# Inverting the sums of the feature maps on ScalarE instead of GpSimd, a start in two halves, and new thresholds in a planned two-part attention kernel

## The chip, the cores and the metric

One core of one Trainium2 chip. The metric is the device time of one launch in microseconds, the median of several runs. Engines are named as in the profile: PE is TensorE, DVE is VectorE, ACT is ScalarE, POOL is GpSimd, and SP is SyncE, whose queue issues nearly all transfers.

## What is computed

Two independent attention layers on inputs of 2048 tokens and 512 features, with 32 heads of 16 features each. The results are laid side by side.

```
# part A: softmax attention
q, k, v = split(x @ wqkv)
p = softmax(q @ k.T / 4)
a = (p @ v) @ wo
# part B: linear attention with a learned feature map
pq, pk = q @ w_phi, k @ w_phi                  # per head, 16 x 16
phi = concat([softmax(pq), softmax(-pq)])      # 16 + 16 features, likewise for pk
kv, z = phi_k.T @ v, sum(phi_k)
b = (phi_q @ kv) / (phi_q @ z + 1e-6) @ wo
out = concat([a, b], -1)
```

## The kernel before

**The planner.** The program is written out by a planner that runs while the kernel is built (`_Account`, L116). It keeps an account of when each engine is free, by costs written into the code (`act_cost`, `dve_cost`, and pairs such as `(1.95, 1.95 + PLAT)` for one task), and at each point of its own time `K.now` it chooses the next instruction for each engine: `pick_pe` (L1927) for PE, `choose` (L1985) for ACT, DVE, POOL and SP, by priority. What comes out is one fixed list for each engine, run in order, with semaphore waits between them (`_Plan.emit`). So an instruction that waits holds up all that stands behind it on its engine, and the costs decide only the order, not the time on the chip.

**Part A** is the bulk. It goes in 73 units (`units`, L230): a group of four heads by 256 (some 128) queries. For each unit the scores are computed twice:

- *D*: scores with the queries on the partitions (`d_fill`, L1041; its matmuls are L971), in PSUM banks of 512 columns. DVE takes the maximum of one or of two banks at once (`tensor_reduce`, L1084), two when a pair of neighbouring banks was free.
- The maxima of a unit are joined (POOL, L1116 to L1122), turned by a transfer and put into spare rows of the masked queries `QZ`, which POOL makes (L915).
- *E*: scores again with the keys on the partitions (`e_fill`, L1215; matmuls L1234), now with the maximum subtracted by the matmul itself. ACT takes the exponential of one or two banks into the ring `pT` (L1246).
- `pv_run` (L1299) multiplies the ring by the values (L1324). `finish_unit` copies the result to `X` (L560), inverts the sums on DVE (L1384) and spreads them by transfers; POOL multiplies (L1403).

A few D items (*z*) are shared: ACT does a relu of 1024 columns (L1011) and DVE a custom instruction (L1078).

**Copies out of PSUM** go through `evac` (L554): some only to ACT, the others to ACT or DVE, whichever is free first. `choose` lets DVE have such a copy only when the work that DVE has left is at most what ACT has left plus the threshold `BAL`.

**The thresholds** (`TH0`, L409, with a row of `TH` for each 60 us of the planner's time) steer `pick_pe`. `SINGLE` is the backlog of DVE, in planned microseconds, below which D may take a single bank though two would be wanted; `ESINGLE` is the same for E on ACT. `DCAP` and `ECAP` are the backlogs above which no more is issued, `COL` and `INCOL` say when PE may turn to the other kinds of matmul, `PV_START`, `PV_LOW` and `PVN` when the ring is emptied. `UA`, `RF`, `REPM`, `LHARD` and `LHI` set how many matmuls are repeated or put in as filler, and `BAL` is told above.

**Part B** is woven into the same lists. `fm(n)` (L1556), for 16 token blocks of keys and then 16 of queries, is a chain: projection on PE, copy to `pB`, seven POOL tasks that find the maximum and minimum of each head (L1588, L1591, L1616) and subtract them, an exponential of 1024 columns on ACT (L1639, tile `eB`), the sums of 16 on POOL (L1645 to L1650, into `rB`, 64 columns of f32), their inverse, and the product `phi` on POOL (L1677). One map's `eB` is used until its `phi` is done (`e_busy`). The inverse of the sums is made by POOL itself: a first guess by integer arithmetic on the bits (L1660), and three Newton steps of three instructions (L1662 to L1664). The guess and the products lie in the tile `WQp`.

**The start.** The weights for the first heads come on ACT's queue, x on SP's in five loads (`load_x`, L328): two of 256 rows and three of 512. PE turns the first 512 rows by 16 matmuls with the identity (L374), when each of the first two loads has landed; DVE and ACT copy them to `xAT` (L381, L383), 512 columns at a time. The first projections of K and Q follow (L710), then `first_qz` (L727) masks Q for the first three units (L734, DVE), and the first D matmuls run. The planner starts its account at 7.6 us.

ACT's table of functions is loaded once, as the set `natural_log_exp_and_others` (L2040).

Of the kernel before, what the change touches and what calls it, by code (L numbers as in the profile page):

```python
# [6 lines left out]
ACT = mybir.ActivationFunctionType  # L7
# [206 lines left out]
def bass_concat_heads__softmax_full_mha__linear_kernel_hedgehog__prompt_kernel(  # L214
# [21 lines left out]
    with contextlib.ExitStack() as es:  # L236
# [91 lines left out]
        def load_x(name, b0, b1):  # L328
            t_xs[name] = P.dma("sp", dsem("xs%d" % name), lambda e: e.dma_start(
                xs[:, b0:b1, :], A_x[0][128 * b0:128 * b1, :].rearrange("(b p) n -> p b n", p=128)))  # L330
# [5 lines left out]
        load_x(2, 4, 8)  # L336
# [27 lines left out]
        t_wqp = pad_copy(WQp, 0, t_wq0)  # L364
# [5 lines left out]

        pe_idle(6, [t_zmv, t_ones])
        for rb in range(4):
            for ct in range(4):
                t_turn = P.op("pe", lambda e, rb=rb, ct=ct: e.matmul(  # L374
                    PS[:, ct, 128 * rb:128 * rb + 128], xs[:, rb, ct * 128:ct * 128 + 128], ident[:, :],
                    start=True, stop=True), [t_xs[rb // 2], t_ident] if ct == 0 else [])
        pe_idle(2)
        t_x0 = []
        for ct in range(4):
            if ct % 2 == 0:  # L380
                t_x0.append(P.op("dve", lambda e, ct=ct: e.tensor_copy(xAT[:, ct, 0:512], PS[:, ct, :]), [t_turn]))  # L381
# [20 lines left out]
        for r in range(4):  # L402
# [11 lines left out]
            {'SINGLE': 1.157, 'UA': 0.408, 'RF': 0.436, 'REPM': 0.215, 'LHI': 0.03, 'PV_START': 5, 'PV_LOW': 5, 'DCAP': 1.302, 'ECAP': 1.815, 'ZBIAS': 0.315, 'BAL': -28.613},  # L414
            {'SINGLE': 0.287, 'UA': 0.425, 'RF': 0.532, 'REPM': 0.196, 'LHARD': 0.35, 'LHI': 0.119, 'DCAP': 1.302, 'ECAP': 1.815, 'ZBIAS': 0.315, 'DBIAS': 0.27, 'BAL': -27.419},
            {'SINGLE': 1.157, 'UA': 0.408, 'RF': 0.436, 'REPM': 0.214, 'LHARD': 0.383, 'LHI': 0.03, 'PV_START': 5, 'PV_LOW': 5, 'PVN': 3, 'DCAP': 1.322, 'ECAP': 1.904, 'ZBIAS': 0.315, 'BAL': -27.335},
            {'COL': 0.708, 'SINGLE': 1.157, 'UA': 0.441, 'REPM': 0.196, 'LHI': 0.065, 'PVN': 3, 'DCAP': 2.495, 'ECAP': 1.461, 'ZBIAS': 0.315, 'DBIAS': 0.27, 'BAL': -27.419},
            {'ESINGLE': 1.165, 'RF': 0.62, 'REPM': 0.196, 'LHI': 0.065, 'ECAP': 1.185, 'ZBIAS': 0.049, 'DBIAS': 0.27, 'BAL': -27.419, 'ZREST': -0.23},
            {'ESINGLE': 1.2, 'RF': 0.62, 'REPM': 0.196, 'LHI': 0.122, 'ECAP': 1.185, 'ZBIAS': 0.049, 'DBIAS': 0.27, 'BAL': -27.419, 'ZREST': -0.23},
            {'COL': 0.63, 'INCOL': 0.753, 'ESINGLE': 1.097, 'RF': 0.436, 'REPM': 0.196, 'LHI': 0.079, 'JOBHOLD': 20.274, 'DCAP': 2.036, 'ECAP': 1.185, 'ZBIAS': 0.034, 'DBIAS': 0.314, 'BAL': -27.419, 'ZREST': -0.23},  # L420
            {'COL': 0.487, 'INCOL': 0.753, 'SINGLE': 0.633, 'ESINGLE': 1.097, 'RF': 0.596, 'REPM': 0.196, 'LHI': 0.079, 'JOBHOLD': 20.274, 'DCAP': 2.036, 'ECAP': 1.185, 'ZBIAS': 0.034, 'DBIAS': 0.334, 'BAL': -27.419, 'ZREST': -0.23},
            {'COL': 0.63, 'INCOL': 0.753, 'SINGLE': 0.663, 'ESINGLE': 1.097, 'UA': 0.458, 'RF': 0.676, 'REPM': 0.196, 'LHARD': 0.355, 'LHI': 0.246, 'JOBHOLD': 14.826, 'PV_START': 5, 'DCAP': 2.036, 'ECAP': 1.276, 'ZBIAS': 0.072, 'DBIAS': 0.278, 'BAL': -30.019, 'ZREST': -0.23},
            {'COL': 0.53, 'INCOL': 0.753, 'SINGLE': 0.674, 'ESINGLE': 1.097, 'UA': 0.442, 'RF': 0.67, 'REPM': 0.369, 'LHARD': 0.317, 'LHI': 0.259, 'JOBHOLD': 12.459, 'PV_START': 5, 'DCAP': 2.021, 'ECAP': 1.276, 'ZBIAS': 0.129, 'DBIAS': 0.278, 'BAL': -37.649, 'ZREST': -0.23},
            {'COL': 0.35, 'INCOL': 0.753, 'SINGLE': 0.749, 'ESINGLE': 1.097, 'UA': 0.433, 'RF': 0.67, 'REPM': 0.369, 'LHI': 0.259, 'JOBHOLD': 25, 'PV_START': 5, 'ECAP': 1.276, 'ZBIAS': 0.391, 'DBIAS': 0.278, 'BAL': -37.649, 'ZREST': -0.23},
# [1656 lines left out]
```

## Time and profile before

| | us |
|---|---|
| median of 3 runs | 1202.8 |
| lowest and highest of them | 1199.12, 1205.19 |
| the profiled execution | 1199.05 |
| its span, first to last instruction | 1197.3 |

The granted clock of TensorE is 0.999 of full speed over the span.

A row of a group reads: line, engine, operation, written tile <- read tiles, shape of both, count | busy us, mean ns of one | us that the engine was idle just before them, and what ended that idle time. Instructions of one engine overlap a little at their ends, so the busy time of many can be less than their count times the mean of one. A row of a timeline begins with the start and the length in us, and puts idle time and what ended it in brackets.

### The profile page before, as it was taken

What the parts mean: (1) busy time and instruction counts of PE and PEld (TensorE: products, weight loads), DVE (VectorE), ACT (ScalarE), POOL (GpSimd) and SP (SyncE); (2) the same over time, 40 slices, a digit from 0 to 9 for tenths busy, and PEclk for the clock granted to TensorE, in tenths of its full rate; (3) what the DMA queues carried; (4) which work ended last, traced back from release to release, by engine and by line L of the source; (5) the groups of instructions that cost most, each with busy time, mean ns of one, the idle gap of its engine ahead of it and who ended that gap; (6) DMA issues with size and microseconds to landing.
All of it is one profiled execution on the core that took longest, in us unless ns stands there. A gap on an engine that the chain in (4) does not pass through costs nothing.

```text
span 1197.3 us, 32106 instructions
## 1 busy us (share of the span) xinstructions
PE 1117.4 (93%) x13025; PEld 468.9 (39%) x13025; DVE 1170.3 (98%) x1290; ACT 1149.8 (96%) x1891; POOL 821.8 (69%) x1636
## 2 busy tenths in 40 slices
PE   8998999998999999999999998999999998899998
PEld 3433333343334333333433333333333333345555
DVE  8999999999999999999999999999999999999995
ACT  5898999999999999999999999999999999999997
POOL 8511211227888888888787887888888888888860
PEclk9999999999999999999999999999999999999999
DMA  5011221210002001001000101121112111111120
GB/s 142 9 25 43 42 48 32 43 38 8 8 14 35 8 6 26 13 10 22 12 7 17 25 7 22 22 49 31 29 34 33 35 34 27 20 29 37 33 30 18
DMA packets 104119, 33.61 MB, mean 28 GB/s; under 512 B 86692, under 2 KB 103972, under 8 KB 103972
## 3 DMA queue, kind: packets, MB, share of 16 engines
q1 hardware_dynamic: 102916, 31.31, 13.4%
q8 instruction: 102, 1.67, 0.6%
q14 instruction: 45, 0.37, 0.1%
q10 hardware_dynamic: 1056, 0.26, 0.1%
HBM read 5.26 MB, written 4.19 MB: 8 GB/s over the span
## 4 chain that ended last, share of the span: by engine, by line
ACT 38%; DVE 33%; PE 23%; SPq 2%; issue 1%; POOL 1%; DMA 1%
ACT pT L1246 32%; DVE part L1084 32%; PE PS L1234 7%; PE PS L971 6%; PE PS L1324 5%; PE PS L1419 2%; ACT eB L1639 1%; ACT xAT L560 1%; PE PS L777 1%; ACT zS L1011 1%; ACT X L560 1%; SPq L1392 1%; ACT WQp L560 1%; POOL uB L1588 1%; PE PS L1563 0%
## 5 line engine op out<-in xcount | busy, mean ns | idle before, releaser
L1084 DVE TENSOR_REDUCE part<-PS 128x2 f32<-128x1024 f32 (+1 forms) x1118 | 1130.0, 1079 | 7.6 <-PE PS L971 5.2
L1246 ACT ACTIVATE pT<-PS 128x512 bf16<-128x512 f32 (+1 forms) x1573 | 1027.7, 797 | 21.3 <-PE PS L1234 17.9
L1234 PE MATMUL PS<-QZ,KT 64*128 64x256 bf16 (+1 forms) x4906 | 560.4, 259 | 40.9 <-ACT pT L1246 22.0
L971 PE MATMUL PS<-KT,QZ 64*128 64x512 bf16 x2139 | 484.5, 383 | 26.3 <-DVE part L1084 9.7
L1234 PEld LDWEIGHTS PS<-QZ,KT 64*128 64x128 bf16 x4906 | 245.5, 94 | 323.1 <-ACT pT L1246 161.4
L971 PEld LDWEIGHTS PS<-KT,QZ 64*128 64x128 bf16 x2139 | 126.2, 93 | 198.2 <-DVE part L1084 72.2
L1324 PE MATMUL PS<-pT,VP 128*17 128x256 bf16 (+1 forms) x4672 | 186.7, 261 | 0.9
L1403 POOL TENSOR_TENSOR QT<-X,Yd 128x256 bf16<-128x256 f32 (+1 forms) x70 | 46.8, 668 | 95.4 <-DMA Yd<-Yd 95.1
L1324 PEld LDWEIGHTS PS<-pT,VP 128*17 128x17 bf16 x4672 | 74.9, 88 | 95.2 <-issue 79.0
L1588 POOL TENSOR_TENSOR uB<-uB 128x256 f32<-128x256 f32 (+2 forms) x160 | 83.4, 522 | 10.1
L1591 POOL TENSOR_SCALAR uB<-uB 128x256 f32<-128x256 f32 (+2 forms) x128 | 82.6, 646 | 11.2
L1116 POOL TENSOR_TENSOR dm<-part 128x16 f32<-128x16 f32 (+1 forms) x66 | 15.7, 238 | 91.1 <-DVE part L1084 90.8
L915 POOL TENSOR_TENSOR QZ<-QT,mask 128x512 bf16<-128x512 bf16 (+1 forms) x70 | 65.9, 941 | 15.7 <-PE PS L1234 12.8
L1645 POOL TENSOR_TENSOR xAT<-eB 128x512 f32<-128x512 bf16 x32 | 36.9, 1152 | 40.8 <-ACT eB L1639 40.6
L1677 POOL TENSOR_TENSOR wA<-eB,rB 128x1024 bf16<-128x1024 bf16 x32 | 61.7, 1928 | 2.0
L560 ACT ACTIVATE xAT<-PS 128x512 f32<-128x512 f32 (+3 forms) x83 | 50.1, 617 | 4.4 <-PE PS L1443 2.9
L1648 POOL TENSOR_TENSOR xAT<-xAT 128x256 f32<-128x256 f32 x64 | 36.0, 563 | 5.0
L1563 PE MATMUL PS<-WKp,xBT 128*128 128x512 bf16 x128 | 36.4, 383 | 1.1 <-ACT pT L1246 0.5
L1639 ACT ACTIVATE eB<-uB 128x1024 bf16<-128x1024 f32 x32 | 36.0, 1124 | 0.0
L1419 PE MATMUL PS<-WOp,QT 128*128 128x512 bf16 x120 | 35.8, 384 | 0.1
L1588 POOL TENSOR_TENSOR uB<-xAT,mB 128x512 f32<-128x512 f32 x32 | 33.8, 1057 | 1.8
L1662 POOL TENSOR_TENSOR WQp<-rB,WQp 128x64 f32<-128x64 f32 x96 | 30.6, 319 | 6.4
(113 smaller groups left out, 752.4 us busy)
## 6 DMA issues: line engine op xcount, KB each, us to landing
out_dram<-xAT SPq DMA_DIRECT2D x31, 128.0 KB, 1.8
Yd<-Yd SPq DMA_DIRECT2D x220, 16.0 KB, 2.1
QT<-eB SPq DMA_DIRECT2D x60, 32.0 KB, 2.0
QZ<-mcols SPq DMA_DIRECT2D x110, 1.0 KB
pT<-in_A_x_dram SPq DMA_DIRECT2D x3, 512.0 KB, 7.5
KT<-eB SPq DMA_DIRECT2D x48, 32.0 KB, 2.0
mcols<-stage SPq DMA_TRANSPOSE x69, 2.2
Yd<-Yd SPq DMA_DIRECT2D x60, 8.0 KB, 1.9
```

What stands on the lines that cost most here:

```text
L560: return P.op("act", lambda e: e.activation(dst, src, ACT.Copy), tk)
L915: "pool", lambda e: e.tensor_tensor(QZ[:, u % NQZ, :, 0:w], QT[:, g, q0:q0 + w].unsqueeze(1).broadcast_to([128, 2, w]), mask2[:, 0, :].uns ...
L971: return e.matmul(PS[:, b, :], QZ[p:p + 64, u % NQZ, r % 2, qt * 128:qt * 128 + 128], KT[p:p + 64, g, kc * 512:(kc + 1) * 512], start=star ...
L1084: tk = P.op("dve", lambda e: e.tensor_reduce(o, banks_ap(banks), AX.X, ALU.max), dep)
L1234: tok = P.op("pe", lambda e, r=rs[k], b=banks[k], kt=kt, x=x: e.matmul(PS[:, b, x * w:(x + 1) * w], KT[64 * (r // 2):64 * (r // 2) + 64, g ...
L1246: tk = P.op("act", lambda e: e.activation(pT[:, s0:s0 + n, :] if n > 1 else pT[:, s0, :], banks_ap(banks), ACT.Exp, scale=0.25), dep)
L1324: tok = P.op("pe", lambda e, r=r, kt=kt, x=x, s=es_[r][1]: e.matmul(PS[32 * r:32 * r + 17, bank, 0:w], VP[:, kt, 4 * g + r, :], pT[:, s, x ...
L1419: return e.matmul(PS[:, b, :], QT[:, i, st * 128:(st + 1) * 128], WOp[:, i, :], start=(i == 0), stop=(i == 7))
L1588: return P.op("pool", lambda e: e.tensor_tensor(o, a, b, op), dep)
L1591: return P.op("pool", lambda e: e.tensor_scalar(o, o, 0.0, None, ALU.max), dep)
L1639: cx["e"] = K.task("act", (0.95, 1.07), lambda eng: P.op("act", lambda e: e.activation(eB[:], uB[:], ACT.Exp), toks(d3)), d3, prio=-0.5, n ...
L1677: cx["phi"] = K.task("pool", (1.95, 1.95 + PLAT), lambda eng: P.op("pool", lambda e: e.tensor_tensor(phiB[k].rearrange("p (g f) -> p g f", ...
```

## The change

Four things change.

- The Newton steps on POOL go. The sums `s_` are overwritten by ACT in place with Ln, then with Exp of the negative: two activations of 64 columns for each of the 32 maps. Each is a task of its own for the planner, with priority -1, ahead of the exponentials of part A (0) and level with the copies (-1).
- The start is done in halves of 256 rows: turn, copy, then the other half, in other banks. Between the halves Q of the first group is projected for the first 256 queries, and masked for the first two units. The copy of the weights of Q moves on DVE behind the first half's copies. The two filler matmuls behind the turn go. The third load of x waits for the landing of the first.
- The planner begins its account at 6.8 us instead of 7.6, knows of PE's work before it, and expects the later weights 0.4 us later.
- The rows of thresholds for all twenty stretches of 60 us are new; the defaults stay.

The diff, with the middle of the table left out:

```diff
-        def load_x(name, b0, b1):
+        def load_x(name, b0, b1, dep=()):
             t_xs[name] = P.dma("sp", dsem("xs%d" % name), lambda e: e.dma_start(
-                xs[:, b0:b1, :], A_x[0][128 * b0:128 * b1, :].rearrange("(b p) n -> p b n", p=128)))
+                xs[:, b0:b1, :], A_x[0][128 * b0:128 * b1, :].rearrange("(b p) n -> p b n", p=128)), list(dep))
...
-        load_x(2, 4, 8)
+        load_x(2, 4, 8, [t_xs[0]])
...
-        t_wqp = pad_copy(WQp, 0, t_wq0)
...
         pe_idle(6, [t_zmv, t_ones])
-        for rb in range(4):
+        t_x0 = {}
+        for hf in range(2):
+            for rb in range(2 * hf, 2 * hf + 2):
+                for ct in range(4):
+                    t_turn = P.op("pe", lambda e, rb=rb, ct=ct, hf=hf: e.matmul(
+                        PS[:, 4 * hf + ct, 128 * (rb % 2):128 * (rb % 2) + 128],
+                        xs[:, rb, ct * 128:ct * 128 + 128], ident[:, :],
+                        start=True, stop=True), [t_xs[hf], t_ident] if ct == 0 else [])
             for ct in range(4):
-                t_turn = P.op("pe", lambda e, rb=rb, ct=ct: e.matmul(
-                    PS[:, ct, 128 * rb:128 * rb + 128], xs[:, rb, ct * 128:ct * 128 + 128], ident[:, :],
-                    start=True, stop=True), [t_xs[rb // 2], t_ident] if ct == 0 else [])
-        pe_idle(2)
-        t_x0 = []
+                dst_x = xAT[:, ct, 256 * hf:256 * hf + 256]
+                src_x = PS[:, 4 * hf + ct, 0:256]
+                if ct % 2 == 0:
+                    t_x0[hf, ct] = P.op("dve", lambda e, o=dst_x, i=src_x: e.tensor_copy(o, i), [t_turn])
+                else:
+                    t_x0[hf, ct] = P.op("act", lambda e, o=dst_x, i=src_x: e.activation(o, i, ACT.Copy), [t_turn])
+            if hf == 0:
+                t_wqp = pad_copy(WQp, 0, t_wq0)
         for ct in range(4):
...
+            t_q0 = P.op("pe", lambda e, ct=ct: e.matmul(
+                PS[:, 0, 0:256], WQp[:, ct, 0, :], xAT[:, ct, 0:256], start=(ct == 0), stop=(ct == 3)),
+                [t_wqp, t_x0[0, 2], t_x0[0, 3]] if ct == 0 else [])
...
-            {'SINGLE': 1.013, 'ESINGLE': 1.026, 'ZBIAS': 0.274, 'DBIAS': 0.27, 'ZREST': 0.238},
-            {'SINGLE': 0.647, 'UA': 0.441, 'RF': 0.465, 'REPM': 0.115, 'PV_LOW': 6, 'DCAP': 2.442, 'ZBIAS': 0.207, 'BAL': 68.611},
-            {'SINGLE': 1.013, 'UA': 0.408, 'REPM': 0.215, 'LHI': 0.119, 'DCAP': 1.302, 'ECAP': 1.815, 'ZBIAS': 0.315, 'DBIAS': 0.27, 'BAL': -28.613},
...
-            {'SINGLE': 1.157, 'UA': 0.408, 'RF': 0.436, 'REPM': 0.214, 'LHARD': 0.383, 'LHI': 0.03, 'PV_START': 5, 'PV_LOW': 5, 'PVN': 3, 'DCAP': 1.322, 'ECAP': 1.904, 'ZBIAS': 0.315, 'BAL': -27.335},
...
-            {'ESINGLE': 1.165, 'RF': 0.62, 'REPM': 0.196, 'LHI': 0.065, 'ECAP': 1.185, 'ZBIAS': 0.049, 'DBIAS': 0.27, 'BAL': -27.419, 'ZREST': -0.23},
...
+            {'COL': 0.405, 'SINGLE': 0.583, 'RF': 0.511, 'LHI': 0.098, 'DCAP': 2.519, 'ECAP': 1.062},
+            {'UA': 0.451, 'JOBHOLD': 14.971},
+            {'SINGLE': 0.565, 'UA': 0.451, 'RF': 0.668, 'LHI': 0.137, 'JOBHOLD': 14.971, 'DBIAS': 0.262, 'ZREST': 0.362},
...
+            {'COL': 0.786, 'SINGLE': 0.284, 'UA': 0.448, 'RF': 0.628, 'REPM': 0.128, 'LHI': 0.137, 'JOBHOLD': 12.341, 'DCAP': 1.2, 'ECAP': 1.415, 'ZBIAS': 0.295, 'DBIAS': 0.388, 'ZREST': 0.268},
...
+            {'COL': 0.639, 'INCOL': 0.639, 'UA': 0.448, 'RF': 0.498, 'LHI': 0.074, 'PV_START': 5, 'ECAP': 1.572, 'DBIAS': 0.201, 'BAL': -27.422},
...
-        K.now = 7.6
+        K.now = 6.8
...
-        T_w2 = K.fixed(t_wa["v"], 9.8)
+        T_w2 = K.fixed(t_wa["v"], 10.2)
...
+        area = [(2.5, 1.9, 1.9), (4.3, 0.6, 0.44), (5.5, 0.6, 0.44), (6.2, 0.45, 0.45)]
...
+                c0 = 256 if (kind, g, c) == ("q", 0, 0) else 0
...
-                        first_qz(b, t)
+                        first_qz(b, t, [2])
...
+        held.add(0)
+        first_qz(0, T_q0, [0, 1])
...
-                nw = wqf[:, 3648:3904].bitcast(F32).rearrange("p (a n) -> p a n", a=2)
-                s_, y_, t_ = rB[:, i, :], nw[:, 0, :], nw[:, 1, :]
...
-                cx["r"] = sm
-                for k in range(3):
-                    c = 1.42 if k == 0 else 1.08
-                    cx["r"] = K.task("pool", (c, c), lambda eng, k=k, d=cx["r"]: newton(k, d.tok), [cx["r"]],
-                                     prio=-1.0, name="newton")
+                s_ = rB[:, i, :]
+                ln = K.task("act", (0.107, 0.22), lambda eng: P.op("act", lambda e: e.activation(
+                    s_, s_, ACT.Ln), [sm.tok]), [sm], prio=-1.0, name="rec")
+                cx["r"] = K.task("act", (0.107, 0.22), lambda eng: P.op("act", lambda e: e.activation(
+                    s_, s_, ACT.Exp, scale=-1.0), [ln.tok]), [ln], prio=-1.0, name="rec")
```

`SINGLE`, where a row names none, is 0.619, `ESINGLE` 0.972 and `BAL` 0.0. `SINGLE` in the rows of 120, 180, 240, 300 and 360 us is 1.013, 1.157, 0.287, 1.157 and 1.157 before, and 0.565, 0.612, 0.284, 0.284 and 0.284 after. `ESINGLE` from 420 us on is between 1.057 and 1.2 before, and between 0.972 and 1.038 after. `BAL` from 120 us on is between -27.3 and -37.6 before; after it is 0.0 up to 420 us, -27.4 to -34.9 up to 960 us, and -33.4 to -63.6 behind.

More of the change, by code (lines that the diff above doesn't have):

```diff
@@ new lines, in bass_concat_heads__softmax_full_mha__linear_kernel_hedgehog__prompt_kernel @@
+            {'ESINGLE': 0.994, 'LHARD': 0.4, 'LHI': 0.123, 'JOBHOLD': 25, 'ECAP': 1.331, 'ZBIAS': 0.4, 'BAL': -34.863, 'ZREST': 0.539},
+            {'SINGLE': 0.706, 'ESINGLE': 0.994, 'REPM': -0.005, 'LHARD': 0.4, 'LHI': 0.123, 'JOBHOLD': 25, 'PV_LOW': 3, 'ECAP': 1.331, 'ZBIAS': 0.4, 'BAL': -33.401, 'ZREST': 0.587},
+            {'ESINGLE': 0.994, 'REPM': 0.056, 'LHARD': 0.4, 'PV_LOW': 3, 'ZBIAS': 0.375, 'BAL': -63.586},
+            {'COL': 0.413, 'SINGLE': 0.457, 'ESINGLE': 0.994, 'REPM': -0.005, 'JOBHOLD': 23.734, 'ECAP': 1.951, 'ZBIAS': -0.189, 'BAL': -33.401, 'ZREST': 0.502},
@@ L431, in bass_concat_heads__softmax_full_mha__linear_kernel_hedgehog__prompt_kernel @@
+            {'ESINGLE': 1.022, 'UA': 0.446, 'RF': 0.467, 'REPM': -0.022, 'LHARD': 0.304, 'PV_START': 5, 'PV_LOW': 4, 'ZBIAS': 0.075, 'DBIAS': 0.195, 'BAL': -63.586},
         ]
@@ L439, in bass_concat_heads__softmax_full_mha__linear_kernel_hedgehog__prompt_kernel @@
         for e in K.free:
-            K.free[e] = 7.6
+            K.free[e] = 6.8
         K.free["pool"] = 14.0
@@ L472, in bass_concat_heads__softmax_full_mha__linear_kernel_hedgehog__prompt_kernel @@
         free_banks = list(range(NBANK))
-        bank_tok = {ct: t_x0[ct] for ct in range(4)}
+        bank_tok = {4 * hf + ct: t_x0[hf, ct] for hf in range(2) for ct in range(4)}
+        free_banks.remove(0)
         pe_mode = [None]
```

66 lines of the change are left out of this document (25 added, 41 removed).

## The prediction

> **What bounds the kernel now.** I first read the busy shares of the page, then the chain of work that ended last, then the busy time by stage.
>
> ```profile
> PE 1117.4 (93%) x13025; PEld 468.9 (39%) x13025; DVE 1170.3 (98%) x1290; ACT 1149.8 (96%) x1891; POOL 821.8 (69%) x1636
> ...
> ACT 38%; DVE 33%; PE 23%; SPq 2%; issue 1%; POOL 1%; DMA 1%
> ```
>
> ```profile
> 60.00:120.00 60.00, 52.81 (x649) 21.08 (x641) 57.95 (x62) 53.84 (x81) 10.53 (x26) 1.00 0.14 34
> 120.00:420.00 300.00, 283.44 (x2937) 111.27 (x2937) 298.65 (x342) 290.61 (x440) 149.82 (x313) 1.00 0.14 28
> 420.00:1140.00 720.00, 674.16 (x7845) 281.77 (x7843) 715.77 (x746) 711.58 (x1221) 601.43 (x1208) 1.00 0.13 24
> ```
>
> The columns after a stage's length are PE, weight loads, DVE, ACT, POOL, then the granted clock, which is full. The chain changes between ACT and DVE, and POOL has 1% of it. By stage, DVE is idle for 1.35 us of 120 to 420 us (300 - 298.65) and 4.2 us of 420 to 1140. ACT is idle for 6.2 us of 60 to 120, 9.4 us of 120 to 420, and 8.4 us of 420 to 1140. So two engines are full, ACT from about 420 us on, DVE all the time, and the end is set by their work plus what stands before and behind it. POOL's 821.8 us are not the limit: GpSimd time taken away pays nothing by itself.
>
> Which of the two is last is seen at the end of the timeline (start, length, engine):
>
> ```profile
> 1180.94 0.17 DVE L1164 TENSOR_REDUCE zS<-part 128x2 bf16<-128x8 f32 x1
> ```
>
> ```profile
> 1176.23 12.21 ACT L1246 ACTIVATE pT<-PS 128x512 bf16<-128x512 f32 x16 [0.29 <-PE PS L1234]
> 1188.86 1.94 ACT L1246 ACTIVATE pT<-PS 128x1024 bf16<-128x1024 f32 x2 [0.41 <-PE PS L1234]
> ```
>
> The last maximum on DVE is done at 1181.1, the last exponential on ACT at 1190.8. ACT ends 9.7 us behind DVE, with 16 pieces in a row and almost no wait. **ACT is late at the end, so the new work lands on the wrong engine of the two**; whether the change pays depends on what ACT gets back.
>
> The profiled execution took 1199.05 us, 1.75 more than its span of 1197.3; the median shown is 1202.8, 3.75 above that. I make the sum against 1199.05 and add 3.75.
>
> **The change, part by part.**
>
> *Newton steps off POOL.* Ten small instructions for each of 32 feature maps go:
>
> ```profile
> L1662 POOL TENSOR_TENSOR WQp<-rB,WQp 128x64 f32<-128x64 f32 x96 | 30.6, 319 | 6.4
> L1663 POOL TENSOR_SCALAR WQp<-WQp 128x64 f32<-128x64 f32 x96 | 23.3, 243 | 8.4
> L1664 POOL TENSOR_TENSOR WQp<-WQp 128x64 f32<-128x64 f32 x64 | 20.4, 319 | 5.3
> L1664 POOL TENSOR_TENSOR rB<-WQp 128x64 f32<-128x64 f32 x32 | 10.2, 319 | 2.7
> L1660 POOL TENSOR_SCALAR WQp<-rB 128x64 int32<-128x64 int32 x32 | 7.8, 243 | 2.7
> ```
>
> 30.6 + 23.3 + 20.4 + 10.2 + 7.8 = 92.3 us of POOL, 2.9 us for each feature map. Since POOL has 1% of the chain, I count 0 for it. What it does bring is that each map's chain is shorter by about 2.9 us less two short activations, so the second part ends earlier; its evacuations then fall earlier on the same ACT, whose total is unchanged.
>
> *64 activations of 64 columns onto ACT.* No row shows this shape. The exponentials of one stage and one small copy bound it:
>
> ```profile
> L1246 ACT ACTIVATE pT<-PS 128x512 bf16<-128x512 f32 x289 | 156.9, 683 | 1.8 <-PE PS L1234 0.7
> L1246 ACT ACTIVATE pT<-PS 128x1024 bf16<-128x1024 f32 x70 | 75.4, 1079 | 1.5 <-PE PS L1234 1.3
> ```
>
> ```profile
> L560 ACT ACTIVATE X<-PS 128x256 f32<-128x256 f32 x55 | 22.1, 401 | 1.4 <-PE PS L1324 1.2
> ...
> L560 ACT ACTIVATE X<-PS 128x128 f32<-128x128 f32 x15 | 5.0, 336 | 0.0
> ```
>
> ```profile
> 520.35 0.42 ACT L560 ACTIVATE X<-PS 128x256 f32<-128x256 f32 x1
> 520.61 6.33 ACT L1246 ACTIVATE pT<-PS 128x1024 bf16<-128x1024 f32 x10
> ```
>
> The first fence is 420 to 660 us. There 512 columns keep ACT for 0.543 us (156.9/289), 1024 for 1.077: 0.534 us per 512 columns and 0.01 fixed, so 64 columns cost at least 0.08. The upper end is a whole duration that overlaps nothing: 336 ns at 128 columns, less half of the 65 ns between 128 and 256, 0.30 us. Between them stands the copy of 256 columns in the timeline, whose successor starts 0.26 us behind it. I take 0.13, half of that row, as the columns are a quarter and something is fixed: 64 x 0.13 = +8.3 us, bounds +5 and +19. The Trainium skill, "ScalarE: Activation LUTs", section "What ACT_TABLE_LOAD costs", gives 186 ns plus 0.833 ns a column, with 93 ns overlapped: an estimate of 0.146 us, by which this term would be +9.4.
>
> *The new wait.* Ln waits for POOL's sums, and behind Ln in ACT's order stand exponentials, for which PE and the ring of probabilities wait. The nearest wait of this kind is that of the activation of line 1639 for POOL's last subtraction:
>
> ```profile
> L1639 ACT ACTIVATE eB<-uB 128x1024 bf16<-128x1024 f32 x32 | 36.0, 1124 | 0.0
> ```
>
> Its 32 instances were idle for 0.0 us: the planner sets them late enough. So I take 0 for Ln. The bound from the other side is the wait in the opposite direction, one step earlier in the same chain:
>
> ```profile
> L1645 POOL TENSOR_TENSOR xAT<-eB 128x512 f32<-128x512 bf16 x32 | 36.9, 1152 | 40.8 <-ACT eB L1639 40.6
> ```
>
> POOL waits there 40.6 us in all for ACT. If ACT waited as long for POOL, it would be +40.6; under 0 it can't be.
>
> *First x in two halves.* The start in the timeline:
>
> ```profile
> 0.79 1.49 SPq L329 DMA_DIRECT2D pT<-in_A_x_dram  x3
> ...
> 4.24 0.65 PE L374 MATMUL PS<-ident,pT 128*128 128x128 bf16 x8
> ...
> 5.47 0.62 PE L374 MATMUL PS<-ident,pT 128*128 128x128 bf16 x8 [0.59 <-DMA pT<-in_A_x_dram]
> 5.84 0.29 DVE L361 COPY WQp<-wA 128x512 bf16<-128x512 bf16 x1 [0.93 <-DMA wA<-in_A_wqkv_dram]
> ...
> 6.13 1.29 DVE L381 CAST xAT<-PS 128x512 bf16<-128x512 f32 x2
> ...
> 7.48 1.04 PE L710 MATMUL PS<-xAT,WKp 128*128 128x512 bf16 x4 [0.95 <-DVE xAT L381]
> ...
> 8.55 0.69 ACT L559 ACTIVATE KT<-PS,bias_k 128x512 bf16<-128x512 f32 x1 [1.34 <-PE PS L710]
> ...
> 9.42 1.35 DVE L734 TENSOR_TENSOR QZ<-PS,mask 128x256 bf16<-128x256 f32 x3 [2.00 <-PE PS L710]
> ...
> 9.98 0.61 PE L971 MATMUL PS<-KT,QZ 64*128 64x512 bf16 x4
> ...
> 10.69 5.74 DVE L1084 TENSOR_REDUCE part<-PS 128x2 f32<-128x1024 f32 x5
> ```
>
> Half 0 is turned by 4.9 us and copied on DVE and ACT before half 1 is turned at 6.1; the WQp copy stays at 5.84. The copies of half 1 take two times about 0.4 us on each engine instead of 0.65, so they end near 6.95, the K projection starts at 7.0 instead of 7.48, and KT is there at 8.75 instead of 9.24. The first half of Q is projected between the halves, so its masking no longer waits till 9.42. The first scores start at 8.8 instead of 9.98: -1.1 us. The cover: the third load of x is now held until the first has landed at 4.2 us, and behind it on SP stand all later loads, issued some 2 us later than now (all three were issued by 2.28). If the third lands after 8.8 us the PE, which works in order, waits, and the 1.1 us are lost. Bounds: -1.2 and +0.5.
>
> *Thresholds.* These decide most, and two can be priced. `SINGLE` lets DVE reduce one bank of 512 when no pair is free; in the four segments of 120 to 240 and 300 to 420 us it falls from 1.013 and 1.157 to between 0.28 and 0.61. The reductions at 120 to 240, 300 to 420 and, with 0.619 already, 420 to 660 us:
>
> ```profile
> L1084 DVE TENSOR_REDUCE part<-PS 128x2 f32<-128x1024 f32 x75 | 88.2, 1214 | 0.8 <-PE PS L971 0.3 <-PE PS L978 0.2
> L1084 DVE TENSOR_REDUCE part<-PS 128x1 f32<-128x512 f32 x53 | 34.6, 676 | 0.0
> ```
>
> ```profile
> L1084 DVE TENSOR_REDUCE part<-PS 128x2 f32<-128x1024 f32 x70 | 81.6, 1211 | 0.1
> L1084 DVE TENSOR_REDUCE part<-PS 128x1 f32<-128x512 f32 x64 | 40.4, 676 | 0.0
> ```
>
> ```profile
> L1084 DVE TENSOR_REDUCE part<-PS 128x2 f32<-128x1024 f32 x198 | 226.4, 1210 | 0.8 <-PE PS L971 0.5
> L1084 DVE TENSOR_REDUCE part<-PS 128x1 f32<-128x512 f32 x12 | 7.8, 682 | 0.0
> ```
>
> Per bank of 512 that is 122.8/203 = 0.605, 122.0/204 = 0.598 and 234.2/408 = 0.574 us. Brought to the third, the first two save 203 x 0.031 + 204 x 0.024 = 11.2 us of DVE. If only the roughly 105 superfluous singles become pairs, it is 52 x (2 x 0.64 - 1.14) = 7.3. I take -9 on DVE.
>
> `ESINGLE`, the same for ACT, falls from between 1.06 and 1.2 to between 0.97 and 1.04 behind 420 us. At 120 to 240 us it is already 0.972:
>
> ```profile
> L1246 ACT ACTIVATE pT<-PS 128x1024 bf16<-128x1024 f32 x74 | 75.3, 1073 | 4.8 <-PE PS L1234 4.8
> L1246 ACT ACTIVATE pT<-PS 128x512 bf16<-128x512 f32 x59 | 34.5, 631 | 0.1
> ```
>
> 109.8/207 = 0.530 us per bank with few singles, against 232.3/429 = 0.541 at 420 to 660 us with 289 of them. That is hardly a gain; I count 0 (the bounds are 0 and 0.011 for each of the some 1,300 banks behind 420 us, -14).
>
> So ACT gets time back mainly from its early idle. If DVE delivers its maxima 9 us sooner by 420 us, the exponentials there find work in the 6.2 + 9.4 = 15.6 us that ACT now idles. I take 9, as many as DVE saves (bounds 0 and 15). With `BAL` at 0 instead of about -28 up to 420 us, DVE may also take some evacuations, each 0.5 to 0.7 us of ACT; I take three, -2 us.
>
> **Sum on ACT, the later engine:** +8.3 - 1.1 - 9 - 2 = -3.8 us. DVE, with -1.1 - 9 + 2 = -8, stays ahead of it. 1199.05 - 3.8 = 1195.2, plus 3.75 = **1199.0 us**.
>
> **The rivals.** *Both engines gain (1191.5).* More evacuations go to DVE, until both share the saving, and the singles behind 1020 us go too: the 11.2 of DVE arrive whole, 1202.8 - 11.3. For it: ACT ends 9.7 us behind DVE, so there is room to share. Against: DVE has only 1.35 us idle at 120 to 420.
>
> *ACT becomes the bound (1210).* Slower: the 64 activations cost 0.13 each and nothing comes back, since ACT is idle for only 8.4 us in the 720 us in which some 50 of them fall, and the early idle is a wait for PE, which is 94% busy there. +8.3 - 1.1 = 1210; at 0.30 each, 1221. It decides as soon as ACT's early idle doesn't shrink by 7 us.
>
> *ACT waits for POOL (1219).* Half of the 40.6 us, 0.6 us at each Ln, on top of the forecast: 1199 + 20.
>
> *The change does nothing (1203).* The third load cancels the start, the thresholds trade waits for singles, and ACT's 8 us go into the early idle.
>
> A table reload at each Ln and Exp would cost 64 x 1.28 us, 82 us, by the one load in the trace:
>
> ```profile
> L2040 ACT ACT_TABLE_LOAD x1 | 1.3, 1283 | 0.8 <-PEq L2066 0.8
> ```
>
> I give it no chance, as the loaded set is named for both functions. The Trainium skill, "ScalarE: Activation LUTs", section "Table sets: the hidden batching unit", lists both in that set; no run here has shown an Ln.
>
> **How the numbers follow.** Forecast 0.38 (1194 to 1204), both gain 0.27, ACT the bound 0.19, nothing 0.10, ACT waits for POOL 0.06. A measurement of this kernel tells about 0.5%, 6 us, from no change. Faster by more (under 1196.8): 0.27 and 0.3 of the forecast, 0.38. Slower by more (over 1208.8): 0.16 of ACT the bound, and 0.06, 0.22. The rest, 0.40, is within. The range 1187 to 1212 leaves out the best of the gains (0.05) and what lies above 1212 (0.13: ACT waiting, and the dearer third of ACT the bound).
>
> **What the changed profile would show.** Right: the first reduction near 9.5 us; fewer than 10 singles per 60 us on DVE at 120 to 420; ACT's idle there under 7 us; 64 activations on rB at about 0.13 us busy with no idle before them; POOL near 730 us. Wrong: idle before the Ln group; the last exponential more than 10 us behind the last maximum; PE waiting for the x load near 8 us; more reductions by ones than now.

## The result and the profile after

| | before | after |
|---|---|---|
| median, 14 runs each | 1201.4 us (1198.66 to 1205.19) | 1206.54 us (1205.87 to 1207.92) |
| ratio after to before | | 1.0043, 95% interval 1.0036 to 1.0051 |
| profiled execution | 1199.05 us, span 1197.3 | 1206.65 us, span 1204.5 |

The change makes the kernel slower by 0.43%, some 5 us. I had called 0.5% either way no change; but the interval is clear of 1, and I had forecast a gain, 1199.0 us against 1202.8.

The page of after, busy times and chain:

```profile
PE 1098.3 (91%) x12959; PEld 456.5 (38%) x13033; DVE 1174.4 (97%) x1249; ACT 1153.1 (96%) x1894; POOL 731.0 (61%) x1316
...
ACT 60%; PE 28%; DVE 8%; POOL 2%; issue 2%; POOLq 0%
```

The stages of after, columns as before (PE, weight loads, DVE, ACT, POOL):

```profile
60.00:120.00 60.00, 53.68 (x632) 21.89 (x631) 60.00 (x65) 54.84 (x87) 10.51 (x26) 1.00 0.15 33
120.00:420.00 300.00, 273.92 (x2865) 106.76 (x2888) 297.88 (x299) 288.45 (x463) 150.50 (x284) 1.00 0.13 28
420.00:1140.00 720.00, 658.07 (x7734) 269.18 (x7773) 710.59 (x742) 711.63 (x1189) 523.03 (x939) 1.00 0.13 25
```

The chain now runs through ACT for 60% and DVE for 8%. ACT's idle time at 60 to 420 us is 5.2 + 11.6 = 16.7 us, against 15.6 before: the early idle that was to pay for the new activations wasn't used. The rise of 1.1 us means nothing: in the four experiments below that keep before's order this idle time is 16.6 to 18.4 us. From 420 to 1140 us DVE is idle for 9.4 us, where before it was 4.2.

The start of after:

```profile
8.31 0.69 ACT L569 ACTIVATE KT<-PS,bias_k 128x512 bf16<-128x512 f32 x1 [1.42 <-PE PS L723]
...
9.08 0.60 PE L986 MATMUL PS<-KT,QZ 64*128 64x512 bf16 x4
...
9.51 4.68 DVE L1099 TENSOR_REDUCE part<-PS 128x2 f32<-128x1024 f32 x5
```

The first reduction is at 9.51 us instead of 10.69. And the reductions of after in the stages that were priced (120 to 240, 300 to 420 and 420 to 660 us):

```profile
L1099 DVE TENSOR_REDUCE part<-PS 128x2 f32<-128x1024 f32 x97 | 111.6, 1213 | 0.8 <-PE PS L986 0.6
L1099 DVE TENSOR_REDUCE part<-PS 128x1 f32<-128x512 f32 x9 | 6.1, 673 | 0.0
```

```profile
L1099 DVE TENSOR_REDUCE part<-PS 128x2 f32<-128x1024 f32 x99 | 113.4, 1210 | 1.0 <-PE PS L986 0.8
L1099 DVE TENSOR_REDUCE part<-PS 128x1 f32<-128x512 f32 x8 | 5.4, 682 | 0.1
```

```profile
L1099 DVE TENSOR_REDUCE part<-PS 128x2 f32<-128x1024 f32 x179 | 206.9, 1213 | 2.3 <-PE PS L986 1.0
L1099 DVE TENSOR_REDUCE part<-PS 128x1 f32<-128x512 f32 x40 | 26.2, 680 | 0.4 <-PE PS L986 0.2
```

The singles went as forecast, from 117 to 17 in the first two; in the third they rose from 12 to 40. But DVE isn't rid of 9 us; its total rose from 1170.3 to 1174.4.

### The profile page after: what moved, and what is told of

It is laid out like the page before. It is cut to its first block, busy times and chain, and to the rows that moved or that the text cites. A ratio compares the mean times of both kernels' runs of the same rounds, so it can differ in the third digit from the quotient of the medians.

```text
span 1204.5 us, 31699 instructions
## 1 busy us (share of the span) xinstructions
PE 1098.3 (91%) x12959; PEld 456.5 (38%) x13033; DVE 1174.4 (97%) x1249; ACT 1153.1 (96%) x1894; POOL 731.0 (61%) x1316
## 4 chain that ended last, share of the span: by engine, by line
ACT 60%; PE 28%; DVE 8%; POOL 2%; issue 2%; POOLq 0%
ACT pT L1261 51%; DVE part L1099 7%; PE PS L1249 7%; PE PS L986 7%; PE PS L1339 7%; ACT xAT L570 2%; ACT eB L1654 2%; PE PS L1434 2%; ACT zS L1026 1%; ACT X L570 1%; PE PS L707 1%; PE PS L790 1%; PE PS L723 1%; ACT WQp L570 1%; ACT vB L570 0%
## 5 line engine op out<-in xcount | busy, mean ns | idle before, releaser
L1249 PE MATMUL PS<-QZ,KT 64*128 64x256 bf16 (+1 forms) x4760 | 540.8, 259 | 50.7 <-ACT pT L1261 32.0
L986 PE MATMUL PS<-KT,QZ 64*128 64x512 bf16 x2063 | 458.0, 383 | 25.6 <-DVE part L1099 10.6
L1249 PEld LDWEIGHTS PS<-QZ,KT 64*128 64x128 bf16 x4760 | 231.4, 94 | 325.5 <-ACT pT L1261 168.7
L986 PEld LDWEIGHTS PS<-KT,QZ 64*128 64x128 bf16 x2063 | 119.7, 93 | 198.7 <-DVE part L1099 67.5
L1339 PE MATMUL PS<-pT,VP 128*17 128x256 bf16 (+1 forms) x4672 | 184.0, 261 | 2.0 <-ACT pT L1261 0.2
L1606 POOL TENSOR_SCALAR uB<-uB 128x256 f32<-128x256 f32 (+2 forms) x128 | 82.6, 645 | 11.2
L570 ACT ACTIVATE xAT<-PS 128x512 f32<-128x512 f32 (+2 forms) x84 | 51.2, 630 | 4.7 <-PE PS L1458 3.2
L1859 PE MATMUL PS<-zmv,ones_t 128*17 128x512 bf16 x328 | 30.5, 387 | 6.6 <-DVE Yd L1371 1.1
L1578 PE MATMUL PS<-WKp,xBT 128*128 128x512 bf16 x104 | 31.4, 382 | 5.3 <-issue 2.7
L1434 PE MATMUL PS<-WOp,QT 128*128 128x512 bf16 x107 | 32.8, 383 | 2.2 <-issue 1.1
L1603 POOL TENSOR_TENSOR uB<-mB,xAT 128x512 f32<-128x512 f32 x32 | 33.8, 1057 | 1.6
```

Source lines behind the costliest of these rows:

```text
L570: return P.op("act", lambda e: e.activation(dst, src, ACT.Copy), tk)
L986: return e.matmul(PS[:, b, :], QZ[p:p + 64, u % NQZ, r % 2, qt * 128:qt * 128 + 128], KT[p:p + 64, g, kc * 512:(kc + 1) * 512], start=star ...
L1249: tok = P.op("pe", lambda e, r=rs[k], b=banks[k], kt=kt, x=x: e.matmul(PS[:, b, x * w:(x + 1) * w], KT[64 * (r // 2):64 * (r // 2) + 64, g ...
L1339: tok = P.op("pe", lambda e, r=r, kt=kt, x=x, s=es_[r][1]: e.matmul(PS[32 * r:32 * r + 17, bank, 0:w], VP[:, kt, 4 * g + r, :], pT[:, s, x ...
L1434: return e.matmul(PS[:, b, :], QT[:, i, st * 128:(st + 1) * 128], WOp[:, i, :], start=(i == 0), stop=(i == 7))
L1603: return P.op("pool", lambda e: e.tensor_tensor(o, a, b, op), dep)
```

## What a small instruction costs: the distance of starts

The reason can be read from ACT's timeline of after, around one Ln and one Exp:

```profile
534.53 2.16 ACT L1261 ACTIVATE pT<-PS 128x512 bf16<-128x512 f32 x3
536.38 0.44 ACT L1671 ACTIVATE rB<-rB 128x64 f32<-128x64 f32 x1
536.53 0.78 ACT L1261 ACTIVATE pT<-PS 128x512 bf16<-128x512 f32 x1
537.01 0.44 ACT L1673 ACTIVATE rB<-rB 128x64 f32<-128x64 f32 x1
537.15 5.68 ACT L1261 ACTIVATE pT<-PS 128x1024 bf16<-128x1024 f32 x7
```

Ln lasts 0.44 us, but its successor starts 0.15 us after it; the exponential of 512 columns lasts 0.78, its successor starts 0.48 after it. Instructions in a row overlap, so a duration overstates what an instruction takes from its engine, and the busy time of the page holds part of the waiting that the overlap covers. I therefore went through the trace by the distance from each start to the next on the same engine. Where nothing is waited for, it is nearly always 0.145 us for 64 columns on ACT, 0.477 for 512 and 0.904 for 1024; on DVE 0.598 for a reduction of one bank and 1.131 for two, though one in fifteen follows 0.02 to 0.05 us sooner (before's first five pairs show the usual distance: 4 x 1.131 + 1.21 = 5.73, and their row says 5.74).

The Trainium skill, "Perfetto Trace Analysis", section "Optimizing Scalar/DVE Operations", says the same of both engines: a profiled duration holds about twice the fixed part that keeps the engine, since the second half overlaps the next instruction. The distances show the fixed part once the columns are taken off: from 512 to 1024 columns ACT takes 0.904 - 0.477 = 0.427 us more, 0.834 ns a column, and DVE 1.131 - 0.598 = 0.533 us. For ACT the page's figures agree with the trace (93 ns for SBUF sources, 0.145 - 64 x 0.000834 = 0.092 us here; 51 ns for PSUM, 0.477 - 0.427 = 0.050 here). For DVE on PSUM it gives about 125 ns, and the reductions here show 0.598 - 0.533 = 0.065 us; the measurement decides. The factor of two is borne out by the shortest durations in after for SBUF sources on ACT (0.248 - 0.053 = 0.195 us) and by the usual ones on DVE (0.680 - 0.533 = 0.147), not for PSUM on ACT (0.588 - 0.427 = 0.161, three times 0.050).

With the distances, two single reductions cost 2 x 0.598 - 1.131 = 0.065 us more than a pair, less than half of the 2 x 0.64 - 1.14 = 0.14 that I took from busy times. All reductions, of before and then of after:

```profile
L1084 DVE TENSOR_REDUCE part<-PS 128x2 f32<-128x1024 f32 x842 | 971.1, 1211 | 6.9 <-PE PS L971 4.8 <-PE PS L978 0.2
L1084 DVE TENSOR_REDUCE part<-PS 128x1 f32<-128x512 f32 x276 | 177.7, 676 | 0.7 <-PE PS L971 0.5
```

```profile
L1099 DVE TENSOR_REDUCE part<-PS 128x2 f32<-128x1024 f32 x890 | 1025.9, 1212 | 10.8 <-PE PS L986 6.9 <-PE PS L993 0.2
L1099 DVE TENSOR_REDUCE part<-PS 128x1 f32<-128x512 f32 x180 | 117.5, 679 | 2.2 <-PE PS L986 0.7 <-PE PS L1249 0.5
```

That is 96 singles less and 48 pairs more: 3.1 us. On the other side stand six copies out of PSUM that DVE takes at 60 to 420 us in after, and none there before (five of 0.6 by distance, one of 0.33), 3.3 us, and more waiting:

```profile
L573 DVE CAST eB<-PS 128x512 bf16<-128x512 f32 x3 | 2.0, 680 | 0.0
L573 DVE CAST WKp<-PS 128x512 bf16<-128x512 f32 x2 | 1.4, 678 | 0.0
L573 DVE COPY X<-PS 128x256 f32<-128x256 f32 x1 | 0.4, 410 | 0.0
```

What the starts lie behind these least distances, summed over the span, was some 26 us on DVE and 85 on ACT before; after it is 35 and 88. Of ACT's 85, 47.5 are idle time on the page (1197.3 - 1149.8); the rest is inside its busy time. DVE's 26 is no more than its idle time on the page, 27.0.

## Experiments

Theory A: the threshold rows are fitted to one exact order of instructions. If one task moves, all later choices come out otherwise, and rows made for another order lose many microseconds; the change is a new, poorer fit. Theory B: the 64 activations load an engine that has no room. Theory C, formed on the way: both, and they can be told apart: the fit makes most of the difference between versions whose rows are of different making, and the activations cost 4 to 8 us where the rows are equally good. Each ratio below is to the kernel before, run beside it (medians of 1201.0 to 1202.0 us).

**One part at a time, the rows kept.** The kernel before with only the Ln and Exp of the diff:

```diff
-                for k in range(3):
-                    c = 1.42 if k == 0 else 1.08
...
+                ln = K.task("act", (0.107, 0.22), lambda eng: P.op("act", lambda e: e.activation(
+                    s_, s_, ACT.Ln), [sm.tok]), [sm], prio=-1.0, name="rec")
...
```

> The kernel before with one part of the change, the inverse by Ln and Exp on ACT; start and thresholds as before. Theory A (fit): the thresholds are fitted to one exact order of instructions; as soon as one task moves, the planner's later choices all come out otherwise, and thresholds made for another order lose 10 to 30 us: 1211 to 1231 us. Theory B (load): the 64 activations start 0.145 us apart from their followers in the trace of after, 9.3 us of an engine that is last at the end: about 1210 us, and the start of after then gives 1 us back and the new thresholds 3. If neither holds, 1201.

Measured 1223.95 us, ratio 1.019 (1.0169 to 1.021). The kernel before with only the start in halves, all hunks of the diff but the rows and the inverse:

```diff
-        for rb in range(4):
...
+        for hf in range(2):
+            for rb in range(2 * hf, 2 * hf + 2):
...
-        K.now = 7.6
+        K.now = 6.8
...
```

> The kernel before with the start in halves alone; Newton steps and thresholds as before. The first reduction at about 9.5 us instead of 10.7. Theory A (fit): the order behind the start comes out otherwise, and the time is 10 to 30 us longer, 1211 to 1231. Theory B (load): nothing is added to ACT, so the 1.2 us of the start arrive, about 1200.

Measured 1225.31 us, ratio 1.02 (1.0184 to 1.0215). And the changed kernel with Newton put back:

```diff
-                ln = K.task("act", (0.107, 0.22), lambda eng: P.op("act", lambda e: e.activation(
...
+                for k in range(3):
+                    c = 1.42 if k == 0 else 1.08
...
```

> The changed kernel with the Newton steps put back on POOL; its start and its thresholds kept. Theory B (load): ACT is rid of 9.3 us, so faster than the changed kernel by up to that, 1197 to 1203. Theory A (fit): these thresholds were made for the order with Ln and Exp, so slower than the changed kernel by 5 to 25 us, 1211 to 1231.

Measured 1214.19 us, ratio to before 1.0107 (1.0092 to 1.0122), so some 8 us slower than the changed kernel, though ACT has 64 activations less. Each part alone costs 2%, both together with new rows 0.4%. Load alone can't do that, since the start adds none to ACT: B is out as the only cause.

**A number without meaning.** The planned length of the product `phi` on POOL, 10 ns longer. Nothing else in the kernel's text changes; what the planner makes of it does, and ACT has 1832 instructions instead of 1891, as more banks go in pairs:

```diff
-                    cx["phi"] = K.task("pool", (1.95, 1.95 + PLAT), ...
+                    cx["phi"] = K.task("pool", (1.96, 1.96 + PLAT), ...
```

> The kernel before with one number of the account changed that has no meaning on the chip: the planned length of the product phi on POOL is 1.96 us instead of 1.95. No instruction is added or removed. Theory A (fit): the order comes out otherwise from the first such product on, and the time is 5 to 25 us longer, 1206 to 1226. If the losses of the other runs came from the work that was moved, this one costs nothing: 1201.

Measured 1209.89 us, ratio 1.0068 (1.0053 to 1.0083): more than the change itself costs. A holds, as far as one such number can show it.

**Where such time goes.** Counted from the rows up to 1020 us, pairs twice, a custom instruction (one z item) four times. The kernel before:

```profile
L1084 DVE TENSOR_REDUCE part<-PS 128x2 f32<-128x1024 f32 x751 | 864.8, 1210 | 5.5 <-PE PS L971 3.5 <-PE PS L978 0.2
L1246 ACT ACTIVATE pT<-PS 128x512 bf16<-128x512 f32 x946 | 528.3, 672 | 3.9 <-PE PS L1234 2.1
L1246 ACT ACTIVATE pT<-PS 128x1024 bf16<-128x1024 f32 x393 | 413.9, 1079 | 15.9 <-PE PS L1234 14.9
L1084 DVE TENSOR_REDUCE part<-PS 128x1 f32<-128x512 f32 x194 | 125.2, 677 | 0.3 <-PE PS L971 0.2
L1078 DVE CUSTOM_DVE_ANT_0 zS<-PS,zS 128x1024 bf16<-128x1024 f32 x22 | 26.7, 1213 | 1.1 <-PE PS L1234 0.7 <-PE PS L971 0.2
```

The kernel before with Ln and Exp alone:

```profile
L1084 DVE TENSOR_REDUCE part<-PS 128x2 f32<-128x1024 f32 x731 | 845.5, 1217 | 8.7 <-PE PS L971 6.0 <-PE PS L978 0.8
L1246 ACT ACTIVATE pT<-PS 128x512 bf16<-128x512 f32 x821 | 466.1, 657 | 3.5 <-PE PS L1234 1.8 <-PE PS L971 0.5
L1246 ACT ACTIVATE pT<-PS 128x1024 bf16<-128x1024 f32 x431 | 449.5, 1071 | 20.7 <-PE PS L1234 18.6 <-PE PS L971 0.2
L1084 DVE TENSOR_REDUCE part<-PS 128x1 f32<-128x512 f32 x221 | 144.3, 682 | 1.0 <-PE PS L971 0.7
L1078 DVE CUSTOM_DVE_ANT_0 zS<-PS,zS 128x1024 bf16<-128x1024 f32 x22 | 26.7, 1215 | 1.2 <-PE PS L971 1.0
```

Before, DVE has reduced 1502 + 194 + 88 = 1784 banks and ACT exponentiated 946 + 786 = 1732: the maxima lead by 52 banks. With Ln and Exp it is 1771 against 1683, 88 banks, DVE a little behind and ACT far behind. The maxima can lead only by some three units (a new unit's masked queries need the place of the fourth before it), and near here the units shrink from 32 banks to 16. So the lead that is allowed halves, and DVE has to stand still until ACT has caught up. The next 60 us, 1020 to 1080, of before and then of Ln and Exp alone:

```profile
1020.00:1080.00 60.00, 54.16 (x796) 25.07 (x796) 59.15 (x66) 59.50 (x92) 50.42 (x112) 1.00 0.14 25
```

```profile
1020.00:1080.00 60.00, 51.27 (x651) 21.36 (x652) 43.07 (x49) 59.99 (x97) 36.68 (x70) 1.00 0.14 28
```

DVE is busy for 59.2 and for 43.1 us, while ACT is full in both. So a large lead at this point is where most of the 22 us of Ln and Exp alone falls due. It is not what makes rows fit or not in general. Counted likewise, the changed kernel's lead is 59, the start alone has 68, and the meaningless 10 ns give 61; but the changed kernel with Newton put back has 51, doesn't stand still here, and is some 12 us slower than before all the same. Its row for 1020 to 1080 us:

```profile
1020.00:1080.00 60.00, 54.70 (x713) 23.50 (x713) 59.55 (x64) 58.88 (x91) 49.30 (x109) 1.00 0.17 28
```

And the start alone loses time long before. Its row for 60 to 120 us, where DVE was busy for 57.95 and ACT for 53.84 us before:

```profile
60.00:120.00 60.00, 53.05 (x686) 20.42 (x684) 52.18 (x58) 47.95 (x68) 9.38 (x25) 1.00 0.14 34
```

What a good set of rows has that another lacks stays open.

**The work itself, at an unchanged order.** To price the move without the fit, I left the planner as it was and changed only what it emits. First Ln and Exp at the places of the first two Newton steps:

```diff
-                    if k == 0:
-                        t = P.op("pool", lambda e: e.tensor_scalar(
...
+                    if k == 0:
+                        return P.op("act", lambda e: e.activation(s_, s_, ACT.Ln), [t])
+                    if k == 1:
+                        return P.op("act", lambda e: e.activation(s_, s_, ACT.Exp, scale=-1.0), [t])
+                    return t
```

> The kernel before, its planner and its order left as they are: where the plan has the first and second Newton step, Ln and Exp are put into ACT's list without the account knowing, and POOL's ten instructions go. So every other instruction of every engine keeps its place, and only the work itself changes engine. Theory B (load): ACT has 64 x 0.145 = 9.3 us more, and the time is about 1210. Theory A (fit): the work itself costs little, since ACT's instructions start on average 0.04 us later than they could and so have room: 1201 to 1205.

Measured 1208.35 us, ratio 1.0053 (1.0032 to 1.0074): 6.4 us by the ratio, between what the two theories expected. Then activations of the same size for which nobody waits, beside the Newton steps:

```diff
+                    if k < 2:
+                        t_dmy[0] = P.op("act", lambda e: e.activation(dmy[:, :], ident[:, 0:64], ACT.Copy), [t_ident, t_dmy[0]])
```

> The kernel before with 64 more activations of 64 columns in ACT's list, at the places of the first and second Newton step, reading a constant and writing a tile that nobody reads; they wait for nothing, the account doesn't know of them, all other instructions keep their place. It tells the load from the wait in the same-order run with Ln and Exp (+6.4 us). Theory B1 (load): 64 x 0.145 us go straight into the time, +6 to +9, 1207 to 1211. Theory B2 (wait): without the waits for POOL's sums nothing is lost, 1200 to 1203.

Measured 1206.72 us, ratio 1.0044 (1.0029 to 1.0059): 5.3 us, a little under what B1 expected. So it is the load, not the wait; the difference of the two is within their intervals. The same on DVE (`e.tensor_copy` in place of the activation):

> The kernel before with 64 more copies of 64 columns in DVE's list at the places of the first and second Newton step, read by nobody, unknown to the account, all else in its place. If DVE is the engine without room (its reductions start on average 0.01 us later than they could, the exponentials 0.04 us): the whole of their time, 64 x 0.1 us and more, +6 to +9. If ACT is the one that is late: under +2. The same size on ACT is run beside it.

Measured 1205.19 us, ratio 1.0032 (1.0021 to 1.0043): 3.8 us, which neither expectation had. By the distance of starts the 64 activations take 9.7 us of ACT and the copies 8.0 us of DVE. About half arrives in each case. That fits two engines of which each is the late one for a part of the time (the chain of before has ACT for 38% and DVE for 33%); it isn't shown where. It speaks against my picture of ACT as the late engine. That picture rested on the 9.7 us between the last maximum and the last exponential. With the 64 activations more on ACT they stand as far apart as before:

```profile
1188.66 0.17 DVE L1165 TENSOR_REDUCE zS<-part 128x2 bf16<-128x8 f32 x1
```

```profile
1196.57 1.94 ACT L1247 ACTIVATE pT<-PS 128x1024 bf16<-128x1024 f32 x2 [0.42 <-PE PS L1235]
```

That is 1198.51 - 1188.83 = 9.68 us; with the copies on DVE it is 9.67, and in after 9.5. So this distance doesn't tell which engine has room. Last, Newton left out and nothing put in its place:

```diff
                 def newton(k, t):
+                    return t
```

> The kernel before without the Newton steps and with nothing in their place, all else in its place; it leaves the inverse out, so the second part multiplies by the sums. It shows what POOL's freed 92 us are worth by themselves at the same order. Both theories: nothing, 1200 to 1203, since POOL has 1% of the chain. If POOL's products were what others wait for, up to 3 us less.

Measured 1201.43 us, ratio 1.0001 (0.9992 to 1.001). The 92 us of POOL are worth nothing.

**All four with rows of one making.** If the rows decide so much, the parts have to be compared with rows that are equally well fitted. I made such rows anew for each combination, by the same search with the same effort. Only the rows differ from the kernel before, from the kernels with one part alone, and from the changed one; the first row of the changed kernel's new set, for instance:

```diff
-            {'COL': 0.405, 'SINGLE': 0.583, 'RF': 0.511, 'LHI': 0.098, 'DCAP': 2.519, 'ECAP': 1.062},
+            {'COL': 0.387, 'SINGLE': 0.583, 'RF': 0.511, 'LHI': 0.098, 'DCAP': 2.519, 'ECAP': 1.062, 'REPM': 0.115},
...
```

> First of four kernels whose threshold rows I found anew by one and the same procedure with the same effort (for each stretch of 60 us, the best of 900 candidates by the planner's account of useful work two stretches on), so that the fit no longer favours one of them. This one: old start, Newton on POOL, the kernel before but for the rows. Theory C (fit and load together): the parts differ by the load alone, so the two with Newton are equal within 4 us, and each with Ln and Exp is 4 to 8 us slower than its partner. Theory A alone (only the fit): no order among the four, all within the scatter of the fit. Here: 1199 to 1206 us.

> Old start, Ln and Exp on ACT, rows found anew by the same procedure. Theory C: 4 to 8 us slower than its partner with Newton, 1205 to 1212; theory A alone: as fast as its partner. Against the run with Ln and Exp under the old rows (1224 us) both expect a gain of 12 us or more.

> Start in halves, Newton on POOL, rows found anew by the same procedure. The start is worth 1.2 us at the first reduction. Theory C: within 4 us of the old start with Newton, 1199 to 1207; theory A alone: anywhere among the four. Against the start in halves under the old rows (1225 us) both expect a gain of 15 us or more.

> Start in halves, Ln and Exp on ACT, rows found anew by the same procedure: the changed kernel but for the rows. Theory C: 4 to 8 us slower than its partner with Newton, 1206 to 1213; theory A alone: as fast as its partner.

| rows made by the same search | Newton on POOL | Ln and Exp on ACT |
|---|---|---|
| old start | 1205.15, ratio 1.0032 (1.0019 to 1.0044) | 1213.81, ratio 1.0104 (1.0088 to 1.0121) |
| start in halves | 1204.06, ratio 1.0029 (1.0018 to 1.004) | 1210.34, ratio 1.0074 (1.0059 to 1.009) |

The ratios are to the kernel before, whose own rows are better than any of these. Between the two columns lie 8.7 and 6.3 us, as theory C expected (4 to 8, once a little more). Between the rows of the table lie 1.1 and 3.5 us in favour of the halves, where 1.2 were expected; a search scatters by a few microseconds, so this is no more than agreement in sign. Rows found anew recover 10.1 us of the 22 that Ln and Exp alone had cost, and 21.3 of the 23.5 of the start.

**A wider search, and a version that beats both.** The first search left 3 us to the rows of the kernel before. So I searched more widely for the two with the start in halves; again only the rows change:

```diff
-            {'UA': 0.451, 'JOBHOLD': 14.971},
+            {'COL': 0.405, 'SINGLE': 0.583, 'RF': 0.511, 'LHI': 0.098, 'DCAP': 2.622, 'ECAP': 1.062, 'REPM': 0.126, 'UA': 0.46},
...
```

> Start in halves and Newton on POOL, with rows from a wider search (eight sets of rows carried along at each stretch of 60 us instead of one, and sets in which the maxima lead by over 56 banks marked down). If a better fit recovers what the first one (1204.1 us) left to the kernel before, 1198 to 1202; the start's 1.2 us then show as at most 0.1%. If the first search was already at its limit, 1203 to 1206.

> Start in halves, Ln and Exp on ACT, the changed kernel but for the rows, which come from the same wider search. Theory C: 3 to 8 us slower than its partner with Newton, as the load stays, so 1202 to 1209. If the 6 us of the first pair were scatter of the search: within 2 us of its partner.

With Newton it is 1199.16 us, ratio 0.9979 (0.9969 to 0.9988): faster than the kernel before by 0.2%, and than the changed one by 0.6%. With Ln and Exp it is 1206.5 us, ratio 1.0041 (1.0026 to 1.0056), no better than the change as it was given. Counted as above, the maxima lead at 1020 us by 51 and 55 banks, so the leads are alike, and still 7.3 us lie between the two. That weighs more than the first two pairs, in which the leads differ: 57 with Newton against 79 with Ln and Exp under the old start, 62 against 83 under the new one.

The distances of starts tell load and fit apart. Take for each shape of instruction on ACT a least distance (the one that a tenth of its distances in all runs lie below), and call the sum of these over a kernel ACT's work. With Ln and Exp the work is longer by 6.1, 4.7 and 6.1 us in the three pairs, in the order in which they were made. What the starts lie behind it differs by 1.2, -1.7 and 1.2 us within a pair, and is 82 to 92 us in all six; in the kernel before it is 84 by this count. In the four kernels whose rows were made for another order (each part alone, Newton put back, the 10 ns) it is 98 to 115. Theory C holds: three pairs made by equal searches give 8.7, 6.3 and 7.3 us for Ln and Exp, and the trace shows most of it as work. The way of searching moves a version by 4 or 5 us (1204.1 to 1199.2, 1210.3 to 1206.5), and the difference within a pair by 1.

## Why the prediction was wrong, step by step

- **Newton off POOL, counted at 0:** right (1.0001 without it). POOL fell from 821.8 to 731.0 us, and that moved nothing.
- **64 activations on ACT, +8.3 us:** right in kind, and as a load nearly right: 0.145 us each by the distance of starts, 9.3 us in all, for which the estimate from the Trainium skill ("ScalarE: Activation LUTs", "What ACT_TABLE_LOAD costs") was closer than mine. What arrives is 5.3 to 6.4 us at the same order, which fits an ACT that is the late engine only part of the time.
- **The new wait, 0:** right. After's rows have 0.2 us of idle before Ln and 0.1 before Exp, and activations that wait and activations that don't cost the same within their intervals.

```profile
L1671 ACT ACTIVATE rB<-rB 128x64 f32<-128x64 f32 x32 | 11.6, 363 | 0.2 <-POOL rB L1665 0.2
L1673 ACT ACTIVATE rB<-rB 128x64 f32<-128x64 f32 x32 | 11.0, 345 | 0.1
```

- **The start, -1.1 us:** right at the first reduction (-1.18; it is at 9.25 to 9.56 us in the seven traces with the new start, at 10.46 to 10.99 in the nine with the old), and the third load of x came in time. The first scores, from which I had worked it out, start only 0.90 us sooner (9.08 instead of 9.98). What of it reaches the end is not shown beyond the sign.
- **SINGLE, -9 us on DVE:** the step that was mis-sized. The singles went, but the term was worked out from busy times, in which overlap and waiting are mixed. By distances it is 3.1 us in the whole kernel, and the copies that DVE took over ate it.
- **ESINGLE, 0:** mis-sized the other way. Exponentials of one bank went from 1098 to 982, of two from 475 to 533; by distances that frees 116 x 0.477 - 58 x 0.904 = 2.9 us of ACT.
- **BAL, -2 us on ACT:** right. Six copies went to DVE; by distances, 0.477 us for each of the five of 512 columns and 0.264 for the one of 256, ACT is rid of 2.6 us.
- **"As many as DVE saves", 9 us of ACT's early idle:** the step that failed, and with it the sign. DVE saved nothing, ACT's early idle did not shrink (15.6 us before, 16.7 after), and without this term my own sum is +8.3 - 1.1 - 2 = +5.2, 1208. That this meets the measured +5.1 is luck in part: by distances ACT's work grew by some 4 us (+9.3 - 2.9 - 2.6 are +3.8), and its starts came some 3 us later behind it.
- **ACT as the late engine at the end, 9.7 us:** a wrong reading. The distance is 9.5 us in after and stays at 9.7 whichever of the two engines gets more work; the sign of being wrong that I tied to it (over 10 us) did not come, and the forecast was wrong all the same.
- **What was missing:** I priced rows of thresholds one by one, as if each kept its effect in another order. What decides there is how well the rows fit the order: rows kept for a changed order cost 0.7 to 2%. None of the rivals was that rows fit one order only. The rival that came nearest is "ACT becomes the bound" (1210), with its own condition: the early idle did not shrink. (In the rival "both engines gain" I subtracted 11.3 where its saving is 11.2; nothing hangs on it.) The table reload, to which I gave no chance, did not occur: after has no load but the one at the start.

## What to carry to other kernels

When an order is made by a planner whose constants were searched for, take a part's price at an unchanged order, and compare versions only with constants searched for equally long; a change of 10 ns in the planner's account moved this kernel by 0.7%. Here, where two engines are nearly full, work added to either arrived by about half, and work taken from a third engine not at all. Price short instructions by the distance to the next start, not by their duration or their share of busy time.

## What I had not expected of the hardware

A reduction of 512 columns on DVE lasts 0.68 us by its row and takes 0.598 from the engine; an activation of 64 columns lasts 0.25 to 0.52 us and takes 0.145. On DVE a copy of 64 columns between SBUF tiles takes 0.10 us by the distance of starts and 0.20 by its duration. ACT is 96% busy by the page, with 47.5 us of idle time, and yet starts its instructions some 85 us later in all than the least distances allow.
